# Two attention branches with a gate on one core: the first phase in another order

## The chip, the cores and the metric

The kernel runs on one core of a Trainium2 chip. The metric is the device time of one execution in microseconds (us); lower is better. PE is the matrix engine (PEld its weight loads), ACT the scalar engine, DVE the vector engine, POOL and SP two more engines, which here mostly issue DMAs.

## The reference

Two attention layers over the same 2048 x 576 input are mixed by a gate. Layer A has 32 heads of 18 columns with keys and values of their own; layer B has 32 query heads that share one key and one value of 18 columns.

```python
x = A_x                                   # 1 x 2048 x 576
g = sigmoid((x * gate_w).sum(-1, keepdims=True))
a = A(x, A_wqkv, A_wo)                    # softmax(q k^T / sqrt(18)) v per head, times wo
b = B(x, B_wq, B_wk, B_wv, B_wo)          # the same, one k and v for all heads
return g * a + (1 - g) * b                # all float32
```

## The kernel before

Products in float32 are built from halves: each operand is split into a rounded part `h` (type fp32r) and the rest `l`, and three of the four products are summed (hh, hl, lh).

The **first phase** multiplies X (transposed, 576 rows in five tiles of 128; the fifth holds the last 64 rows twice, the second copy being the rest of the split) by a matrix `wall` of 14 tiles of 128 columns, which holds key, gate, value and queries of layer B and queries and keys of layer A. X has four chunks of 512 columns. One pair of weight tile and chunk is one **bank** (`project`, one PSUM bank `ps`): 14 matmuls in the order of the list `PROJ`, 56 banks in all. ACT evicts a bank into `ph`, DVE the rest into `pl`; `ph` is stored to DRAM (`qkh`) by a DMA that ACT issues, `pl` (`qkl`) by one that POOL issues. `ph` and `pl` have three buffers each. For tiles with keys, the difference of the first two chunks is split and stored as well (`kdh`, `kdl`).

The input loads are issued by SP: `load5` brings a tile with 576 rows in three DMAs (512 rows, and the last 64 twice). First the small store of `ones` to DRAM, the first weight tile (`wst`), four X loads of 256 columns (`xs`), the second weight tile, four more X loads, four weight tiles. `split_x` makes `xh` on ACT and `xl` on DVE of 256 columns; `prep_w` makes `wh` and `wl` of a weight tile. For each chunk, tiles 0 and 1 are projected; behind them `shared_v` transposes the value of layer B on PE (L174). `project_rest` then takes tiles 2 to 13, four chunks each.

Rows of `qkh`, `qkl` and `kdh`, `kdl` are read back as operands of the attention: `ksb` and `kdb` (the shared key), `qs` (three buffers for the queries of three heads). The loads of `ksb`, `kdb` and the first head stand together on POOL behind the first eight banks in the program, those of the second and third heads behind tiles 4 and 5.

A **lead** follows the first phase: the value projection (`project_v`, L187) and the first row maxima (`step_max`, L341 and L350). Then comes the long second part, a fixed order of scores (L376), exponentials (L383), and products with the values (L390), with output projections in between. The order of the instructions of each engine is that of the program text; nothing is reordered.

Of the kernel before, what the change touches and what calls it, by code (L numbers as in the profile page):

```python
# [22 lines left out]
NKT = 5  # L23

MT = 14
ROW_KB, ROW_G, ROW_VB, ROW_Q = 0, 18, 32, 50
SCALE = DH ** -0.5
LEAD = 22
PRODS = (("h", "h"), ("h", "l"), ("l", "h"))
PROJ = [("h", "h", k, 128) for k in range(NKT)] + [("h", "l", k, 128) for k in range(NKT - 1)] + \  # L30
       [("l", "h", k, 128) for k in range(NKT)]


def q_row(u):
    return ROW_Q + DH * u if u < H else ROW_Q + DH * H + 2 * DH * (u - H)
# [7 lines left out]
def gated_mix_kernel(ctx: ExitStack, tc: tile.TileContext, xT, wall, wv, wo, out):  # L43
    nc = tc.nc
    P = 128

    def dma(o, i, eng=None):
        o, i = (x.bitcast(F32) if x.dtype == F32R else x for x in (o, i))
        return (eng or nc.sync).dma_start(o, i)  # L49
# [4 lines left out]
    ps_m = ctx.enter_context(tc.tile_pool(name="ps_m", bufs=4, space=PSUM))  # L54
# [4 lines left out]
    qk_d = [dram.tile([MT * P, S], F32, name=f"qk{x}") for x in "hl"]  # L59
    kd_d = [dram.tile([MT * P, 512], F32, name=f"kd{x}") for x in "hl"]  # L60
# [20 lines left out]
    nc.vector.memset(acc, 0.0)  # L81
    nc.vector.memset(vb, 1.0)
    nc.vector.memset(ones, 1.0)
    dma(ones_r.rearrange("a (b c) -> (a b) c", c=32), ones)

    SB, MB = 0, 64

    def load_rows(t, r, parts, eng=None):  # L90
        for b in (MB, SB):
            for i, y in enumerate(parts):
                dma(t[b + 18 * i:b + 18 * i + 18, :], qk_d[y][r:r + 18, :], eng)

    def load_q(u, eng=None):
        load_rows(qs[u % 3], q_row(u), (0, 0, 1), eng)

    def load_kd(t, r, eng=None):
        for i, y in enumerate((0, 1, 0)):
            dma(t[MB + 18 * i:MB + 18 * i + 18, :], kd_d[y][r:r + 18, :], eng)  # L100

    def load_k(t, r, eng=None):
        load_rows(t, r, (0, 1, 0), eng)


    ph1 = ExitStack()
# [1 line left out]
    wpool = ph1.enter_context(tc.tile_pool(name="wpool", bufs=2, side="right"))  # L108
    stp = ph1.enter_context(tc.tile_pool(name="stp", bufs=3, side="right"))
    X = {"h": xpool.tile([P, NKT, S], F32R, name="xh"), "l": xpool.tile([P, NKT - 1, S], F32R, name="xl")}  # L110
# [6 lines left out]
        if l is not None:  # L117
            eng_l.tensor_tensor(l, src, h.bitcast(F32), op=OP.subtract)

    def load5(t, src):  # L120
        dma(t[:, 0:4, :], src[0:512, :].rearrange("(k p) m -> p k m", p=P))
        dma(t[0:64, 4, :], src[512:576, :])
        dma(t[64:128, 4, :], src[512:576, :])

    def split_w(st, w, eng_l):
        nc.scalar.activation(w["h"], st, AF.Copy)
        eng_l.tensor_tensor(w["l"], st, w["h"].bitcast(F32), op=OP.subtract)

    def load_w(mt):
        st = wpool.tile([P, NKT, P], F32, name="wst", bufs=6)  # L130
        load5(st, wall[mt])
        return st

    def prep_w(st):
        w = {y: wpool.tile([P, NKT, P], F32R, name=f"w{y}") for y in "hl"}
        split_w(st, w, nc.vector)
        return w

    HAS_K = {0} | {k_row(u) // P for u in range(H, NU)} | {(k_row(u) + DH - 1) // P for u in range(H, NU)}
    KD = {}  # L140

    def project(mt, c, w):

        fp = ps_s.tile([P, 512], F32, name="ps")
        cs = slice(c * 512, (c + 1) * 512)
        for n, (a, b, k, kr) in enumerate(PROJ):
            nc.tensor.matmul(fp, w[a][:kr, k, :], X[b][:kr, k, cs], start=(n == 0), stop=(n == len(PROJ) - 1))  # L147
        h = stp.tile([P, 512], F32R, name="ph")
        l = stp.tile([P, 512], F32R, name="pl")
        nc.scalar.activation(h, fp, AF.Copy)  # L150
        if mt == 0 or c == 0 and mt in HAS_K:
            st = stp.tile([P, 512], F32, name="pst", bufs=3)
            nc.scalar.activation(st, fp, AF.Copy)
            if c == 0:
                KD[mt] = st
        nc.vector.tensor_tensor(l, fp, h.bitcast(F32), op=OP.subtract)  # L156
# [27 lines left out]
    def project_v(st_, hf, w):  # L184
        fp = ps_s.tile([P, 512], F32, name="ps")
        for n, (a, b, k, kr) in enumerate(PROJ):
            nc.tensor.matmul(fp[:, 0:288], X[b][:kr, k, st_ * P:(st_ + 1) * P], w[a][:kr, k, :],  # L187
                             start=(n == 0), stop=(n == len(PROJ) - 1))
        t = vst[st_ % 3]
# [3 lines left out]
    def run(gen):  # L193
        for _ in gen:
            pass

    WV = []
    with tc.tile_pool(name="xs", bufs=6, side="right") as xsp:
        W = [load_w(0)]
        XS = []  # L200

        def load_x(c):
            XS.append(xsp.tile([P, NKT, 256], F32, name="xs"))
            load5(XS[c], xT[:, 256 * c:256 * c + 256])

        def split_x(c):
            xs = XS[c]
            cs = slice(c * 256, (c + 1) * 256)
            xh = X["h"][:, :, cs]
            nc.scalar.activation(xh, xs, AF.Copy)  # L210
            nc.vector.tensor_tensor(X["l"][:, :, cs], xs[:, 0:4], xh[:, 0:4].bitcast(F32), op=OP.subtract)
            nc.vector.tensor_tensor(xh[64:128, 4], xs[64:128, 4], xh[64:128, 4].bitcast(F32), op=OP.subtract)

        for c in range(4):
            load_x(c)
        W.append(load_w(1))
        for c in range(4, 8):
            load_x(c)
        for mt in range(2, 6):
            W.append(load_w(mt))  # L220
        WP = [prep_w(W.pop(0))]
        for c in range(2):
            split_x(c)
        WP.append(prep_w(W.pop(0)))
        for c in range(4):
            if c < 3:
                split_x(2 * c + 2)
                split_x(2 * c + 3)
            keep = project(0, c, WP[0])
            project(1, c, WP[1])  # L230
            shared_v(*keep)
    vwp = ph1.enter_context(tc.tile_pool(name="vwp", bufs=1, side="right"))
    VS = [vwp.tile([P, NKT, 288], F32, name="vwst"), None]
    load5(VS[0], wv[:, 0:288])

    for b in (SB, MB):
        dma(ksb[b + 54:b + 56, :], ones_r, nc.gpsimd)
    load_k(ksb, ROW_KB, nc.gpsimd)
    load_kd(kdb, ROW_KB, nc.gpsimd)
    load_q(0, nc.gpsimd)  # L240

    def project_rest():
        WN = prep_w(W.pop(0))
        for mt in range(2, MT):
            w = WN
            if mt + 1 < MT:
                WN = prep_w(W.pop(0))
            if mt + 4 < MT:
                W.append(load_w(mt + 4))
            for c in range(4):  # L250
                project(mt, c, w)
            if mt in (4, 5):
                load_q(mt - 3, nc.gpsimd)
            if mt in (8, 11):
                hf = (mt - 8) // 3
                WV.append({y: vwp.tile([P, NKT, 288], F32R, name=f"vw{y}{hf}") for y in "hl"})
                split_w(VS[hf], WV[hf], nc.vector)
                if hf == 0:
                    VS[1] = vwp.tile([P, NKT, 288], F32, name="vwst")
                    load5(VS[1], wv[:, 288:576])  # L260

    project_rest()


    small = ctx.enter_context(tc.tile_pool(name="small", bufs=1, side="left"))
# [350 lines left out]
    for T in range(-LEAD, NSTEP + 2, 2):  # L616
# [9 lines left out]
        for op in (LEADS if T < 0 else FIRST if T == 0 else ALONE if alone else UNIT if units else PLAIN).split():  # L626
            k, second, c = op[0], op[1:2] == "B", op[2:]
# [67 lines left out]
```

## Time and profile before

| | |
|---|---|
| median of three runs | 2796.87 us (2795.1 to 2798.84) |
| the profiled execution | 2797.98 us, span 2795.9 us |
| PE, DVE, ACT busy | 99%, 87%, 87% of the span |
| mean granted PE clock | 0.995 |
| instructions | 57640 |

In the rows of a timeline the first number is the start, the second the length, both in us, then engine, line, operation, the tiles written and read, and how many were merged; in brackets stands the idle time ahead and what ended it. In a list of waits stand the sum, how often, and the longest. In rows on DMA issues the last number is the median time from issue to landing.

### The profile page before, as it was taken

To read this page: it belongs to the slowest core of one execution; us is meant where nothing else is said; L and a number is where in the kernel's file an instruction comes from. 1 tells how busy PE (TensorE), PEld (TensorE's weight loads), DVE (VectorE), ACT (ScalarE), POOL (GpSimd) and SP (SyncE) were. 2 spreads that over 40 slices of the span, in tenths; PEclk is the share of its full clock that TensorE was granted. 3 is DMA by queue.
4 is the path that set the end of the run, shared out by engine and by line. 5 is a ranking of instruction groups with operands and counts; after the bars stand their busy time and mean duration, and the time that the engine had idled before them with its cause. 6 is when DMAs were issued, how large, how long until landed. Compare 5 with 4: busy or idle time off the path is not lost.

```text
span 2795.9 us, 57640 instructions
## 1 busy us (share of the span) xinstructions
PE 2767.0 (99%) x22140; PEld 1229.2 (44%) x22140; DVE 2431.6 (87%) x4524; ACT 2430.6 (87%) x4768; POOL 207.2 (7%) x364
## 2 busy tenths in 40 slices
PE   7999999999999999999999999999999999999999
PEld 5888433333333333333333444444444443334544
DVE  3346999999999999999999999899898999998865
ACT  3231899999999999999999999999999999998775
POOL 2220000001001000100110001000100011001000
PEclk9999999999999999999999999999999999999999
DMA  8662011111112111211143223232232323233412
GB/s 258 221 230 76 27 33 33 31 47 51 40 26 57 55 32 32 64 47 26 45 101 106 70 74 104 61 85 76 80 84 76 79 71 84 63 95 107 103 36 92
DMA packets 137143, 215.09 MB, mean 77 GB/s; under 512 B 55437, under 2 KB 94301, under 8 KB 125182
## 3 DMA queue, kind: packets, MB, share of 16 engines
q1 hardware_dynamic: 116156, 168.13, 22.6%
q10 hardware_dynamic: 14120, 22.30, 2.2%
q0 software_dynamic: 6592, 20.99, 2.2%
q8 instruction: 174, 2.85, 0.4%
q14 instruction: 101, 0.83, 0.1%
HBM read 137.31 MB, written 64.77 MB: 72 GB/s over the span
## 4 chain that ended last, share of the span: by engine, by line
PE 94%; DMA 3%; DVE 2%; issue 0%; SPq 0%; ACT 0%; POOL 0%; DVEq 0%; ACTq 0%; POOLq 0%
PE ps L376 40%; PE acc L390 38%; PE ps L147 5%; PE pm L341 5%; PE pm L506 4%; PE ps L187 2%; DVE mx L350 1%; DMA xs<-xT 1%; DVE oacc L560 0%; DMA qkl<-pl 0%; SPq L49 0%; DMA ksb<-qkl 0%; DMA qs<-qkh 0%; DMA ksa<-qkh 0%; DVE oacc L514 0%
## 5 line engine op out<-in xcount | busy, mean ns | idle before, releaser
L383 ACT ACTIVATE pt<-ps 128x512 f32<-128x512 f32 x4052 | 2128.6, 612 | 108.2 <-PE pm L341 45.6
L350 DVE TENSOR_REDUCE mx<-pm 128x1 f32<-128x512 f32 x3096 | 1975.9, 683 | 168.0 <-PE pm L341 126.7
L376 PE MATMUL ps<-qs,ksb 56*128 56x512 f32 x2688 | 908.2, 437 | 0.0
L341 PE MATMUL pm<-ksb,qs 54*128 54x512 f32 x2364 | 825.5, 446 | 1.1 <-DVE mx L350 0.3
L376 PEld LDWEIGHTS ps<-qs,ksb 56*128 56x128 f32 x2688 | 437.0, 184 | 685.2 <-ACT pt L383 665.1
L390 PE MATMUL acc<-pt,vb 128*19 128x256 f32 (+1 forms) x6144 | 592.5, 457 | 0.1
L390 PE MATMUL acc<-pt,vg 128*19 128x256 f32 (+1 forms) x5656 | 579.3, 481 | 0.7 <-DVE oe L400 0.4
L376 PE MATMUL ps<-qs,ksa 56*128 56x512 f32 x1364 | 455.7, 437 | 0.0
L341 PE MATMUL pm<-ksa,qs 54*128 54x512 f32 x1232 | 433.5, 443 | 0.0
L341 PEld LDWEIGHTS pm<-ksb,qs 54*128 54x128 f32 x2364 | 379.5, 184 | 10.6 <-DVE mx L350 4.1
L376 PEld LDWEIGHTS ps<-qs,ksa 56*128 56x128 f32 x1364 | 218.2, 184 | 342.9 <-ACT pt L383 316.8
L347 DVE CUSTOM_DVE_ANT_0 junk<-pm,xb 128x512 bf16<-128x512 f32 x500 | 339.9, 680 | 0.0
L344 ACT ACTIVATE xb<-pm 128x512 f32<-128x512 f32 x500 | 305.1, 610 | 0.0
L341 PEld LDWEIGHTS pm<-ksa,qs 54*128 54x128 f32 x1232 | 200.3, 184 | 0.9
L390 PEld LDWEIGHTS acc<-pt,vb 128*19 128x19 f32 x6144 | 104.2, 97 | 209.9 <-issue 199.9
L390 PEld LDWEIGHTS acc<-pt,vg 128*19 128x19 f32 x5656 | 95.9, 97 | 209.0 <-issue 197.7
L341 PE MATMUL pm<-kdb,qs 54*128 54x512 f32 x372 | 148.6, 400 | 0.0
L116 POOL CAST mh<-mt 128x32 fp32r<-128x32 f32 x64 | 13.4, 209 | 1683.4 <-DVE mt L358 1683.4
L156 DVE TENSOR_TENSOR pl<-ps,ph 128x512 fp32r<-128x512 f32 x56 | 38.4, 690 | 98.1 <-ACT ph L150 70.2
L150 ACT ACTIVATE ph<-ps 128x512 fp32r<-128x512 f32 x56 | 33.4, 597 | 102.4 <-PE ps L147 87.4
L147 PE MATMUL ps<-xh,wh 128*128 128x512 f32 x280 | 75.6, 401 | 20.9 <-ACT xh L210 13.4
L147 PE MATMUL ps<-xh,wl 128*128 128x512 f32 x280 | 73.5, 393 | 0.0
(99 smaller groups left out, 1334.7 us busy)
## 6 DMA issues: line engine op xcount, KB each, us to landing
qs<-qkh SPq DMA_DIRECT2D x244, 144.0 KB
qs<-qkl SPq DMA_DIRECT2D x122, 144.0 KB
qkh<-ph ACTq DMA_DIRECT2D x56, 256.0 KB
qkl<-pl POOLq DMA_DIRECT2D x56, 256.0 KB, 3.1
ksa<-qkh SPq DMA_DIRECT2D x88, 144.0 KB
onh<-oh SPq DMA_DIRECT2D x32, 256.0 KB
onl<-ol SPq DMA_DIRECT2D x32, 256.0 KB
oih<-onh SPq DMA_DIRECT2D x16, 512.0 KB
```

The lines of the kernel that those rows point to most:

```text
L147: nc.tensor.matmul(fp, w[a][:kr, k, :], X[b][:kr, k, cs], start=(n == 0), stop=(n == len(PROJ) - 1))
L150: nc.scalar.activation(h, fp, AF.Copy)
L156: nc.vector.tensor_tensor(l, fp, h.bitcast(F32), op=OP.subtract)
L187: nc.tensor.matmul(fp[:, 0:288], X[b][:kr, k, st_ * P:(st_ + 1) * P], w[a][:kr, k, :], start=(n == 0), stop=(n == len(PROJ) - 1))
L341: nc.tensor.matmul(pm, qs[u % 3][b:b + 54, i * P:(i + 1) * P], k, start=True, stop=True)
L344: nc.scalar.activation(MX["x", u, i], pm, AF.Relu)
L347: nc.vector.tensor_tensor_reduce(junk, pm, MX.pop(("x", u, i)), 1.0, -3e38, op0=OP.add, op1=OP.max, accum_out=MX[u][:, i, c:c + 1])
L350: nc.vector.tensor_reduce(MX[u][:, i, c:c + 1], pm, axis=AX.X, op=OP.max)
L376: nc.tensor.matmul(ps, kst(u)[b:b + 56, i * P:(i + 1) * P], qs[u % 3][b:b + 56, c * 512:(c + 1) * 512], start=True, stop=True)
L383: nc.scalar.activation(pt, ps, AF.Exp, scale=SCALE)
L390: nc.tensor.matmul(acc[32 * j:32 * j + 19, a:b], v_of(u, i), PT[u, i, j][:, a:b], start=(i == 0), stop=(i == 15), skip_group_check=True)
L506: nc.tensor.matmul(fp[:, 0:288], o[b][:r, t, s2 * P:(s2 + 1) * P], w[a][:r, t, 288 * hf:288 * hf + 288], start=(n == 0), stop=(n == 3 * nt ...
```

## The change

- `PROJ` has the order hh, lh, hl for the first four row tiles, and the fifth at the end. `load5` maps row 4p+k instead of 128k+p to partition p of row tile k, for X, `wall` and `wv` alike.
- The first weight tile is issued by ACT, behind a copy of `ones` onto itself on ACT; the first X load is SP's first DMA; the small parts of the second X load and of the second weight tile, and the third weight tile, are issued by POOL. The store of `ones` is issued behind the X loads. X is loaded in two pieces of 256 columns and three of 512.
- Three weight tiles instead of two are projected for each chunk, and `wh` and `wl` have three buffers. The split of the next chunk stands behind the second tile. The first bank is computed in two halves of 256 columns.
- Five matmuls of 304 columns on the identity and a constant tile are put ahead of the first bank; their result is not used.
- The row loads of `ksb`, `kdb` and the first three heads are put into a list, and one is issued on POOL behind each bank from tile 3 on. The load of `wv` moves to tile 5.

```diff
-PROJ = [("h", "h", k, 128) for k in range(NKT)] + [("h", "l", k, 128) for k in range(NKT - 1)] + \
-       [("l", "h", k, 128) for k in range(NKT)]
+PROJ = [(a, b, k, 128) for a, b in (("h", "h"), ("l", "h"), ("h", "l")) for k in range(NKT - 1)] + \
+       [("h", "h", NKT - 1, 128), ("l", "h", NKT - 1, 128)]
...
-    dma(ones_r.rearrange("a (b c) -> (a b) c", c=32), ones)
+    nc.scalar.activation(ones, ones, AF.Copy)
...
-    def load5(t, src):
-        dma(t[:, 0:4, :], src[0:512, :].rearrange("(k p) m -> p k m", p=P))
-        dma(t[0:64, 4, :], src[512:576, :])
-        dma(t[64:128, 4, :], src[512:576, :])
+    def load5(t, src, eng=None, rest=None):
+        dma(t[:, 0:4, :], src[0:512, :].rearrange("(p k) m -> p k m", p=P), eng)
+        dma(t[0:64, 4, :], src[512:576, :], rest or eng)
+        dma(t[64:128, 4, :], src[512:576, :], rest or eng)
...
-        for n, (a, b, k, kr) in enumerate(PROJ):
-            nc.tensor.matmul(fp, w[a][:kr, k, :], X[b][:kr, k, cs], start=(n == 0), stop=(n == len(PROJ) - 1))
+        g = 512 // parts
+        for i in range(parts):
+            for n, (a, b, k, kr) in enumerate(PROJ):
+                nc.tensor.matmul(fp[:, g * i:g * i + g], w[a][:kr, k, :],
+                                 X[b][:kr, k, c * 512 + g * i:c * 512 + g * i + g],
+                                 start=(n == 0), stop=(n == len(PROJ) - 1))
...
+    warm = ps_m.tile([P, 512], F32, name="pm")
+    for i in range(5):
+        nc.tensor.matmul(warm[:, 0:304], ident, vst[0].rearrange("p h d -> p (h d)"), start=True, stop=True)
+    rows_back = []
+    def bring_row():
+        if rows_back:
+            rows_back.pop(0)()
+    def later(o, i, eng):
+        rows_back.append(lambda: dma(o, i, nc.gpsimd))
...
-        for c in range(4):
-            load_x(c)
-        W.append(load_w(1))
-        for c in range(4, 8):
-            load_x(c)
-        for mt in range(2, 6):
+        W = [load_w(0, nc.scalar)]
+        load_x(0)
+        load_x(1, nc.gpsimd)
+        W.append(load_w(1, nc.scalar, nc.gpsimd))
+        W.append(load_w(2, nc.gpsimd))
+        for c in range(2, 5):
+            load_x(c)
+        dma(ones_r.rearrange("a (b c) -> (a b) c", c=32), ones)
+        for mt in range(3, 6):
             W.append(load_w(mt))
         WP = [prep_w(W.pop(0))]
-        for c in range(2):
-            split_x(c)
+        split_x(0)
+        split_x(1)
+        WP.append(prep_w(W.pop(0)))
         WP.append(prep_w(W.pop(0)))
         for c in range(4):
+            keep = project(0, c, WP[0], 2 if c == 0 else 1)
+            if c == 3:
+                WN = prep_w(W.pop(0))
+            project(1, c, WP[1])
             if c < 3:
                 split_x(2 * c + 2)
                 split_x(2 * c + 3)
-            keep = project(0, c, WP[0])
-            project(1, c, WP[1])
             shared_v(*keep)
+            project(2, c, WP[2])
...
-    load_k(ksb, ROW_KB, nc.gpsimd)
-    load_kd(kdb, ROW_KB, nc.gpsimd)
-    load_q(0, nc.gpsimd)
+    load_k(ksb, ROW_KB, put=later)
+    load_kd(kdb, ROW_KB, put=later)
+    for u in range(3):
+        load_q(u, put=later)
...
+        for mt in range(3, MT):
...
+            if mt == 5:
+                load_wv(0)
             for c in range(4):
                 project(mt, c, w)
-            if mt in (4, 5):
-                load_q(mt - 3, nc.gpsimd)
+                bring_row()
```

More of the change, by code (lines that the diff above doesn't have):

```diff
@@ L83, in gated_mix_kernel, with load_rows, load_q, load_kd @@
     nc.vector.memset(ones, 1.0)
-    dma(ones_r.rearrange("a (b c) -> (a b) c", c=32), ones)
+    nc.scalar.activation(ones, ones, AF.Copy)
     SB, MB = 0, 64
-    def load_rows(t, r, parts, eng=None):
+    def load_rows(t, r, parts, put=dma):
         for b in (MB, SB):
             for i, y in enumerate(parts):
[L93 to L98, printed above, removed]
+                put(t[b + 18 * i:b + 18 * i + 18, :], qk_d[y][r:r + 18, :], None)
+    def load_q(u, put=dma):
+        load_rows(qs[u % 3], q_row(u), (0, 0, 1), put)
+    def load_kd(t, r, put=dma):
         for i, y in enumerate((0, 1, 0)):
-            dma(t[MB + 18 * i:MB + 18 * i + 18, :], kd_d[y][r:r + 18, :], eng)
-    def load_k(t, r, eng=None):
-        load_rows(t, r, (0, 1, 0), eng)
+            put(t[MB + 18 * i:MB + 18 * i + 18, :], kd_d[y][r:r + 18, :], None)
+    def load_k(t, r, put=dma):
+        load_rows(t, r, (0, 1, 0), put)
     ph1 = ExitStack()
@@ L127, in split_w, with load_w @@
         eng_l.tensor_tensor(w["l"], st, w["h"].bitcast(F32), op=OP.subtract)
-    def load_w(mt):
+    def load_w(mt, eng=None, rest=None):
         st = wpool.tile([P, NKT, P], F32, name="wst", bufs=6)
-        load5(st, wall[mt])
+        load5(st, wall[mt], eng, rest)
         return st
     def prep_w(st):
-        w = {y: wpool.tile([P, NKT, P], F32R, name=f"w{y}") for y in "hl"}
+        w = {y: wpool.tile([P, NKT, P], F32R, name=f"w{y}", bufs=3) for y in "hl"}
         split_w(st, w, nc.vector)
@@ L140, in gated_mix_kernel, with project @@
     KD = {}
-    def project(mt, c, w):
+    def project(mt, c, w, parts=1):
         fp = ps_s.tile([P, 512], F32, name="ps")
         cs = slice(c * 512, (c + 1) * 512)
-        for n, (a, b, k, kr) in enumerate(PROJ):
-            nc.tensor.matmul(fp, w[a][:kr, k, :], X[b][:kr, k, cs], start=(n == 0), stop=(n == len(PROJ) - 1))
+        g = 512 // parts
[4 more added lines that the diff above has]
+                                 start=(n == 0), stop=(n == len(PROJ) - 1))
         h = stp.tile([P, 512], F32R, name="ph")
@@ L195, in run, with load_x @@
             pass
+    warm = ps_m.tile([P, 512], F32, name="pm")
[7 more added lines that the diff above has]
+        rows_back.append(lambda: dma(o, i, nc.gpsimd))
     WV = []
-    with tc.tile_pool(name="xs", bufs=6, side="right") as xsp:
-        W = [load_w(0)]
+    VS = [None, None]
+    with tc.tile_pool(name="xs", bufs=1, side="right") as xsp:
         XS = []
-        def load_x(c):
-            XS.append(xsp.tile([P, NKT, 256], F32, name="xs"))
-            load5(XS[c], xT[:, 256 * c:256 * c + 256])
+        def load_x(c, rest=None):
+            half = c < 2
+            XS.append(xsp.tile([P, NKT, 256 if half else 512], F32, name=f"xs{half}", bufs=2))
+            load5(XS[c], xT[:, 256 * c:256 * c + 256] if half else xT[:, 512 * (c - 1):512 * c], None, rest)
         def split_x(c):
-            xs = XS[c]
+            xs = XS[c // 2 + 1][:, :, 256 * (c % 2):256 * (c % 2) + 256] if c > 1 else XS[c]
             cs = slice(c * 256, (c + 1) * 256)
@@ L228, in gated_mix_kernel, with load_wv, project_rest @@
                 split_x(2 * c + 3)
-            keep = project(0, c, WP[0])
-            project(1, c, WP[1])
             shared_v(*keep)
+            project(2, c, WP[2])
     vwp = ph1.enter_context(tc.tile_pool(name="vwp", bufs=1, side="right"))
-    VS = [vwp.tile([P, NKT, 288], F32, name="vwst"), None]
-    load5(VS[0], wv[:, 0:288])
+    def load_wv(hf):
+        VS[hf] = vwp.tile([P, NKT, 288], F32, name="vwst")
+        load5(VS[hf], wv[:, 288 * hf:288 * hf + 288])
     for b in (SB, MB):
-        dma(ksb[b + 54:b + 56, :], ones_r, nc.gpsimd)
-    load_k(ksb, ROW_KB, nc.gpsimd)
-    load_kd(kdb, ROW_KB, nc.gpsimd)
-    load_q(0, nc.gpsimd)
-    def project_rest():
-        WN = prep_w(W.pop(0))
-        for mt in range(2, MT):
+        later(ksb[b + 54:b + 56, :], ones_r, None)
+    load_k(ksb, ROW_KB, put=later)
+    load_kd(kdb, ROW_KB, put=later)
+    for u in range(3):
+        load_q(u, put=later)
+    def project_rest(WN):
+        for mt in range(3, MT):
             w = WN
@@ L247, in project_rest @@
                 WN = prep_w(W.pop(0))
-            if mt + 4 < MT:
-                W.append(load_w(mt + 4))
+            if mt + 3 < MT:
+                W.append(load_w(mt + 3))
+            if mt == 5:
+                load_wv(0)
             for c in range(4):
                 project(mt, c, w)
-            if mt in (4, 5):
-                load_q(mt - 3, nc.gpsimd)
+                bring_row()
             if mt in (8, 11):
@@ L258, in project_rest @@
                 if hf == 0:
-                    VS[1] = vwp.tile([P, NKT, 288], F32, name="vwst")
-                    load5(VS[1], wv[:, 288:576])
-    project_rest()
+                    load_wv(1)
+        assert not rows_back
+    project_rest(WN)
     small = ctx.enter_context(tc.tile_pool(name="small", bufs=1, side="left"))
```

## The prediction

> **What bounds the kernel now.** I read the page's busy times first, then the table of windows, the timeline of each engine where PE is idle, the chain, and the waits and DMA issues of single stretches.
>
> ```profile
> PE 2767.0 (99%) x22140; PEld 1229.2 (44%) x22140; DVE 2431.6 (87%) x4524; ACT 2430.6 (87%) x4768; POOL 207.2 (7%) x364
> ```
>
> ```profile
> 0.00:13.36 13.36, 0.00 (x0) 0.00 (x1) 3.33 (x7) 4.56 (x4) 1.56 (x9) 1.00 0.58 180
> ...
> 71.67:207.49 135.82, 135.82 (x590) 112.29 (x591) 52.22 (x73) 43.85 (x70) 34.60 (x65) 0.98 0.65 226
> 207.49:2795.90 2588.41, 2581.51 (x21341) 1077.75 (x21339) 2352.10 (x4410) 2361.49 (x4665) 155.76 (x261) 1.00 0.24 64
> ```
>
> In the windows the first number is the length, the second PE's busy time. PE is idle for 28.9 us (2795.9 - 2767.0), and 13.4 of these lie before the first matmul; from 71.67 to 207.49 it never stops. The first phase (56 banks of 14 matmuls, L147) ends at 207.49, where the chain goes over to the first L187 matmul (its row stands below). The change touches nothing behind that point, so I ask only when the first phase ends after it.
>
> PE at its own pace needs this for a bank:
>
> ```profile
> 47.52 1.45 PE L147 MATMUL ps<-xh,wh 128*128 128x512 f32 x5 [2.73 <-ACT wh L126]
> ```
>
> ```profile
> 71.67 2.50 PE L147 MATMUL ps<-xh,wh 128*128 128x512 f32 x5 [4.78 <-DVE pl L156]
> ...
> 77.22 1.30 PE L147 MATMUL ps<-xh,wh 128*128 128x512 f32 x5
> ```
>
> ```profile
> 118.47 1.30 PE L147 MATMUL ps<-xh,wh 128*128 128x512 f32 x5
> ```
>
> From 77.22 to 118.47 are 13 banks: 3.173 us each, so 56 banks are 177.7 us. The first phase lasts 29.8 us longer than that. The bank at 71.67 takes 5.55 us (to 77.22), 2.4 too many, after 4.78 us idle; the one at 47.52, after 2.73 us idle, runs at the usual pace. So an idle PE loses its clock somewhere between these two lengths and pays 2.4 us to get it back.
>
> ```profile
> 13.36 2.51 PE L147 MATMUL ps<-xh,wh 128*128 128x512 f32 x5 [13.36 <-ACT xh L210]
> ...
> 19.05 1.33 PE L147 MATMUL ps<-xh,wh 128*128 128x512 f32 x5
> ...
> 22.71 1.43 PE L147 MATMUL ps<-xh,wh 128*128 128x512 f32 x5
> ```
>
> The first bank lasts from 13.36 to 19.05, 2.5 us over the pace. The next, with a transpose group behind it, ends at 22.71: 3.66, so a group costs 0.5, four of them 2.0. The 29.8 us are then: start 13.4, two cold banks 4.9, the stall at 66.89 4.8, the wait for the third weight tile at 47.52 2.7, transposes 2.0, and 2.0 left for small waits for splits.
>
> **The start.** These are SP's issues and its wait ahead of the first, then ACT, then DVE, up to 14 us:
>
> ```profile
> 1.83 0.35 SPq L49 DMA_DIRECT2D ones_r<-ones  x1
> 2.24 1.75 SPq L49 DMA_DIRECT2D wst<-wall  x3
> 4.03 7.55 SPq L49 DMA_DIRECT2D xs<-xT  x12
> ```
>
> ```profile
> SPq L49 <- DVE ones L83: 1.2, 1, 1.2
> ```
>
> ```profile
> 5.96 1.28 ACT L126 ACT_TABLE_LOAD   x1 [5.96 <-DMA wst<-wall]
> 7.25 0.74 ACT L126 ACTIVATE wh<-wst 128x640 fp32r<-128x640 f32 x1
> 8.81 1.27 ACT L210 ACTIVATE xh<-xs 128x1280 fp32r<-128x1280 f32 x1 [0.82 <-DMA xs<-xT]
> 12.04 1.27 ACT L210 ACTIVATE xh<-xs 128x1280 fp32r<-128x1280 f32 x1 [1.96 <-DMA xs<-xT]
> ```
>
> ```profile
> 1.71 0.09 DVE L83 MEMSET ones<- 128x32 f32 x1
> 8.02 0.82 DVE L127 TENSOR_TENSOR wl<-wst,wh 128x640 fp32r<-128x640 f32 x1 [6.22 <-ACT wh L126]
> 10.11 1.23 DVE L211 TENSOR_TENSOR xl<-xs,xh 128x1024 fp32r<-128x1024 f32 x1 [1.27 <-ACT xh L210]
> 11.37 0.42 DVE L212 TENSOR_TENSOR xh<-xs,xh 64x256 fp32r<-64x256 f32 x1
> ```
>
> SP waits 1.2 us for the memset of ones before its first issue, then issues the first weight tile, and reaches X only at 4.03; the first X tile has landed 4.78 us later, at 8.81. Without that wait it could begin with X at 0.6; I take 0.9, so it can land at 5.7. The weight tile is issued by ACT, behind the copy of ones (memset ends at 1.80, copy short, table load beside it): about 2.4. Before it took 3.7 us from 2.24 to 5.96, so now it lands at 6.1. The table load (1.28) no longer stands behind that. ACT: weights 6.1 to 6.9, first half of X 6.9 to 8.2. ACT also issues the second weight tile in between, which as built waits for the first X load; that is there by then. First real matmul 8.3 instead of 13.36, since the first bank is now two halves of 256 columns, and only half of X is needed. Bounds: 7.5, if the loads land a microsecond earlier than before for lack of a queue ahead of them; and 10.1, the end of the present xh at 8.81, if three queues bring nothing earlier.
>
> What the halves cost shows in the chain's row of matmuls with 288 columns and weights of the same shape:
>
> ```profile
> 207.49 3.70 PE ps L187 x28
> ```
>
> 0.132 us each, so 14 with 256 columns are at most 1.85 us, a pair of halves 3.7 instead of 3.17. But the second half waits for its own data. DVE has wl, xl, the lower tile, xl, the lower tile (0.82, 1.23, 0.42, 1.23, 0.42) from 6.9 on: with ACT's first half ending at 8.2, the first xl ends at 9.4, and the new order of PROJ puts the products with xl behind eight others, so the first half bank runs from 8.3 to 10.3. The small parts of the second X tile come by Pool's queue:
>
> ```profile
> 1.24 0.93 POOL L182 MEMSET vst<- 128x304 f32 x3
> ```
>
> ```profile
> L49 POOL DMA_DIRECT2D qkl<-pl x41 | 22.2, 541 | 86.1 <-DVE pl L156 86.0 <-issue 0.2
> ```
>
> Pool is free at 2.2 and issues two in 1.1 us; with the 5.9 us from issue to landing that this queue needs at a moderate load (row below) they are there at 9.2, with the 11.2 of its worst row below at 14.5. I take 5.9, since little else is on the queue yet: ACT copies from 9.2 to 10.5, xl ends at 11.7, the lower tile at 12.1, and bank one at 12.5, against 19.05. With 14.5 it ends at 17.7 (1.27, 1.23, 0.42 and the last two matmuls behind it), the late bound.
>
> The idle matmuls are five plain float32 ones of 304 columns on identity and a memset tile. The nearest row:
>
> ```profile
> L390 PE MATMUL acc<-pt,vb 128*19 128x256 f32 (+1 forms) x6144 | 592.5, 457 | 0.1
> ```
>
> 457 ns for 256 columns gives 543 ns for 304, and twice that at the slow clock: 2.7 to 5.4 us from about 1.6 on, over by 7.0 at the latest. So they stand in nobody's way and leave 1 to 4 us idle before 8.3. By the two gaps above (2.73 kept the clock, 4.78 lost it) the first bank should find a fast clock in most cases: 2.4 us saved, 0 at worst.
>
> The Trainium skill, "TensorE: Matmul & The Clock Gate", Part 1, says that the clock is gated to half until one window of about 3.4 us has been busy, and is gated again after an idle one, the windows running free. The trace agrees: 3.4 lies between 2.73 and 4.78. By this rule a gap over 3.4 us here would make the matmuls useless; that is a rival below.
>
> **Three tiles a chunk.** A chunk of 512 columns of X now feeds three banks, 9.5 us and a transpose, instead of two, 6.3. Between chunks PE needs two ACT copies (2.54), two pairs on DVE (3.3) and the evictions. ACT does the copies behind the eviction of the second tile, so they run beside the third bank: they end at 12.5 + 3.2 + 0.6 + 0.3 + 2.5 = 19.1, and the third bank, with a transpose group ahead of it, at 19.3. The lower halves come 2 us later, but the order of PROJ needs them 1.8 us after the bank begins. So at most some tenths for each of three chunks. Weight tiles two and three are prepared before the first bank, tile four at chunk 3, two banks ahead of its use: the 2.73 us at 47.52 goes.
>
> What can come late are the loads of X:
>
> ```profile
> DMA  9999999999999999899798999989999285059999
> GB/s 343 261 272 270 346 320 345 354 326 376 348 361 335 307 284 323 237 277 274 251 303 198 354 340 397 478 277 292 376 422 347 75 314 182 23 205 220 234 285 306
> DMA packets 6246, 6.51 MB, mean 296 GB/s; under 512 B 530, under 2 KB 5026, under 8 KB 6245
> ```
>
> That is the DMA view from 20 to 42 us, in 40 slices: the 16 DMA engines are full (9 tenths or more) in most. Up to the last X tile (needed near 36) come 5.2 MB of X, 1.0 MB of weights and some 4.2 MB of stores: 10.4 MB, at 296 GB/s 35 us, from 2.4 on: 37.6, 1.6 us late. The new loads have longer pieces (rows p*4+k are neighbours, so a weight piece is 2 KB instead of 512 B, X of a whole chunk 2 KB instead of 1 KB), so I expect more than 296. I take 1.0 us for all waits in this stretch, bounds 0 and 6.
>
> **Rows for the lead.** Now 17 loads (2 of ones, 6 and 3 of the shared key, 6 of the first head) stand in a row on Pool, ahead of the stores of pl of the next banks:
>
> ```profile
> DVE pl L156 <- DMA qkl<-pl: 12.2, 1, 12.2
> ...
> PE ps L147 <- DVE pl L156: 4.8, 1, 4.8
> ```
>
> DVE waits 12.2 us for a buffer of pl, PE therefore 4.8, plus 2.4 cold. With one load behind each bank of tile 3 and on, 29 of them, Pool issues a store, then one row. The nearest rows are the loads of two heads at 95 and 108 us, six in a row on the same queue (DMA view from 93 to 120 us):
>
> ```profile
> qkl<-pl POOLq DMA_DIRECT2D x8, 256.0 KB, 5.7
> qs<-qkh POOLq DMA_DIRECT2D x8, 144.0 KB, 5.9
> ```
>
> PE never stops there (fully busy from 71.67 to 207.49). As built, each Pool load waits for the one eight before it. With a store, a row and a quarter of kdl a bank, eight last 3.173 * 8 / 2.25 = 11.3 us; 5.9 is well inside. The stall of 7.2 us goes at no cost; all rows come from tile 0 and are in by tile 10. Loads of weights and of wv are early as before.
>
> **The sum.** Bank one ends at 12.5. The other 55 banks: 174.5. Transposes 2.0, waits 1.0, and 0.6 for the bank after a transpose, which starts 0.14 slower (1.43 against 1.30). End of the first phase 190.6 instead of 207.49: 16.9 us less. The profiled execution took 2797.98 us (span 2795.9), so 2781.1; its time lies 1.1 over the median 2796.87, from which it would be 2780.0. I forecast 2780.
>
> **The rivals.** A: the data comes late. By the Trainium skill, "DMA: Bandwidth & Descriptors", Issuing engines are not separate DMA queues, loads issued from several engines share the same 16 DMA engines, and it only saves the issuing time. As a mechanism here: the three first issuers only share out what SP alone moved, the second X tile lands at 12.04 as now and the first bank ends at 15 (1.27, 1.23 and 0.42 later) instead of 12.5, and the X tiles at the 296 GB/s of the row come 1.6 us late twice: 2.5 + 3.2 = 5.7, so 2786. For it speak the full slices from 20 us on; against it that the DMA share before 13.36 is only 0.58 (last but one number of the first window) and that SP reaches X at 4.03. If one wait passes 3 to 4 us, 2.4 for the clock comes on top: 2788.
>
> B: the idle matmuls do not hold the clock (over too early, at 4.3, and the first bank late). Cost 2.4: 2783. For it: 543 ns at full speed would end them by 4.3, four microseconds before 8.3; against: they begin cold.
>
> C, slower: the rows spread over 29 banks hold up each bank, not only one spell. If a load on Pool's queue takes longer than 11.3 us, Pool is late with each next store, DVE waits for pl and PE for the bank. To be slower by over 5.6 us it must eat 16.9 + 5.6 = 22.5 us, 0.78 a bank, so loads must take (3.17 + 0.78) * 8 / 2.25 = 14.0 us. From there on it is over 2802.5. For it: in the present burst (DMA view from 46 to 72 us) a load took this:
>
> ```profile
> kdb<-kdl POOLq DMA_DIRECT2D x1, 36.0 KB, 11.2
> ```
>
> Against: 5.9 at the pace of a few in between, and PE unharmed by six in a row.
>
> D: the second part gives it back. It is ordered by hand and its engines wait for nothing of the first; I see no row for that, but a remainder.
>
> **How the numbers follow.** Forecast 0.62, with its own range 2776 to 2783; A 0.2 (2784 to 2789); B 0.1; C 0.03; D 0.05, of which most within 0.2%. 0.2% is 5.6 us, about what a measurement of this kernel can tell from no change (runs from 2795.1 to 2798.84). Early bound: start at 7.5 and no waits, 1.8 us less than the sum, and as much again for the runs' own spread (1.8 below the median): 2776. The forecast's own range, B and most of A lie up to 2788. Faster by more than 0.2% needs only 5.6 of the 16.9 us: the forecast, A, B, and a little of D, 0.93; same 0.04; slower 0.03.
>
> **What would show it.** In the profile after: first L149 matmul near 8.3; tile 0's second half done near 12; no idle PE over 1 us from there to the first L191 matmul near 190; that one bank in three has the transposes; DVE's wait for qkl stores gone; from L191 on the same length to the end, 2588.4 us. Wrong would be: PE idle for pl between 45 and 140 us (C), ACT idle for xs at the second or third chunk (A), a first bank in matmuls of 0.2 us and more after the data is there (B), or a longer rest behind the first L191 (D).

## The result, and the profile after

The changed kernel takes 2792.67 us (median of 22 runs, 2790.59 to 2795.58) against 2797.04 us before (22 runs): ratio 0.9984, 95% interval 0.9978 to 0.999. It is faster by 4.4 us; 2780 had been forecast. The profiled execution (2795.58 us) was the slowest of the 22.

The table of windows of the changed kernel, cut where PE stops and where the first phase ends (the last three numbers of a row are PE's granted clock, the busy share of the DMA engines and GB/s):

```profile
0.00:11.84 11.84, 4.73 (x11) 3.00 (x11) 1.68 (x5) 3.46 (x5) 5.43 (x16) 0.88 0.78 254
11.84:17.01 5.17, 5.17 (x28) 5.17 (x29) 4.50 (x6) 2.47 (x3) 0.00 (x0) 0.62 1.06 284
17.01:34.40 17.39, 17.39 (x80) 13.31 (x78) 8.61 (x13) 7.03 (x10) 3.27 (x6) 1.00 0.67 214
34.40:40.35 5.95, 0.00 (x1) 0.00 (x1) 1.18 (x1) 2.48 (x3) 0.00 (x0) 0.94 0.83 316
40.35:60.39 20.04, 20.04 (x79) 15.64 (x79) 10.16 (x16) 7.29 (x11) 2.70 (x5) 0.85 0.64 207
60.39:203.43 143.04, 143.04 (x632) 118.49 (x633) 54.07 (x76) 46.67 (x75) 44.60 (x83) 1.00 0.71 243
203.43:2793.80 2590.37, 2583.37 (x21341) 1080.43 (x21339) 2352.00 (x4410) 2361.72 (x4665) 155.84 (x261) 0.99 0.24 64
```

The first phase ends at 203.43 instead of 207.49: 4.06 us, close to the 4.4 of the medians. The rest takes 2590.4 against 2588.4; over all profiles of this document its length lies between 2587.7 and 2590.4. The stall at 66.89 is gone: PE is busy throughout from 40.35 to 203.43. The second window shows the first bank at a granted clock of 0.62. A stop of 5.95 us at 34.40 is new, and the bank behind it is slow: it lasts from 40.35 to 46.49, 6.1 us where a bank at pace takes 3.2. The timeline of PE marks both stops:

```profile
1.64 4.73 PE L204 MATMUL pm<-vst,ident 128*128 128x304 f32 x10 [1.64 <-POOL vst L186]
11.84 1.22 PE L149 MATMUL ps<-xh,wh 128*128 128x256 f32 x4 [5.47 <-ACT xh L230]
40.35 2.08 PE L149 MATMUL ps<-xh,wh 128*128 128x512 f32 x4 [5.95 <-ACT xh L230]
...
46.49 1.09 PE L149 MATMUL ps<-xh,wh 128*128 128x512 f32 x4
```

Both waits are for xh, a copy of ACT. ACT's timeline ahead of the first one (rows of ACTq are DMAs that ACT issues):

```profile
1.84 0.39 ACTq L49 DMA_DIRECT2D wst<-wall  x1
...
9.89 0.74 ACT L126 ACTIVATE wh<-wst 128x640 fp32r<-128x640 f32 x1 [7.65 <-DMA wst<-wall]
10.53 2.41 ACT L230 ACTIVATE xh<-xsTrue 128x1280 fp32r<-128x1280 f32 x2
```

The first weight tile, issued at 1.84, is there at 9.89: 8.0 us, where the prediction had 3.7 us and a landing at 6.1. Ahead of the second stop:

```profile
30.00 0.33 ACTq L49 DMA_DIRECT2D qkh<-ph  x1
30.60 0.33 ACTq L49 DMA_DIRECT2D kdh<-pdh  x1
30.97 0.34 ACTq L49 DMA_DIRECT2D z_d<-pst  x1
31.41 0.60 ACT L154 ACTIVATE ph<-ps 128x512 fp32r<-128x512 f32 x1 [0.83 <-PE pm L178]
37.43 0.33 ACTq L49 DMA_DIRECT2D qkh<-ph  x1
37.87 2.43 ACT L230 ACTIVATE xh<-xsFalse 128x1280 fp32r<-128x1280 f32 x2 [5.86 <-DMA qkh<-ph]
```

ACT has evicted the bank at 32.0 and then does nothing until 37.43, when it issues the store of that bank; the copies of the next chunk stand behind it in its order. The chain names what ended that wait, the store issued at 30.00:

```profile
30.00 7.36 DMA qkh<-ph
37.87 2.44 ACT xh L230 x2
```

That store is there at 37.36 (30.00 + 7.36), and the issue behind it starts at 37.43. In the program as built, the two stores share one of eight completion counters, and an issue waits until the DMA that used its counter last has landed (ACT's instructions, numbered in its order):

```
24 L49 DMACopy qkh<-ph 128x512 [waits DMAHW5_49,Activation_49]
...
28 L49 DMACopy qkh<-ph 128x512 [waits DMAHW5_49,Activation_49]
29 L230 Activation xh<-xsFalse 128x5x256 [waits DMAHW4_49,DMAHW3_49]
```

### The profile page after: what moved, and what is told of

Read it like the earlier page. It is cut to its first block, busy times and chain, and to the rows that moved or that the text cites. A ratio compares the mean times of both kernels' runs of the same rounds, so it can differ in the third digit from the quotient of the medians.

```text
span 2793.8 us, 57690 instructions
## 1 busy us (share of the span) xinstructions
PE 2773.7 (99%) x22164; PEld 1236.0 (44%) x22164; DVE 2432.2 (87%) x4524; ACT 2431.1 (87%) x4769; POOL 211.8 (8%) x371
## 4 chain that ended last, share of the span: by engine, by line
PE 96%; DVE 2%; DMA 1%; ACT 0%; SPq 0%; issue 0%; DVEq 0%; POOL 0%; ACTq 0%
PE ps L406 41%; PE acc L420 38%; PE ps L149 6%; PE pm L371 5%; PE pm L536 4%; PE ps L191 2%; DVE mx L380 1%; DVE oacc L590 0%; DMA qs<-qkl 0%; DVE oacc L544 0%; DMA xsTrue<-xT 0%; DMA qkh<-ph 0%; PE pm L406 0%; SPq L49 0%; DMA qs<-qkh 0%; DVE oe L430 0%
## 5 line engine op out<-in xcount | busy, mean ns | idle before, releaser
L149 PE MATMUL ps<-xh,wh 128*128 128x512 f32 (+1 forms) x285 | 85.1, 397 | 11.4 <-ACT xh L230 11.4
L149 PE MATMUL ps<-xh,wl 128*128 128x512 f32 (+1 forms) x285 | 83.8, 392 | 0.0
```

The costliest lines, as they stand in the source:

```text
L149: nc.tensor.matmul(fp[:, g * i:g * i + g], w[a][:kr, k, :], X[b][:kr, k, c * 512 + g * i:c * 512 + g * i + g], start=(n == 0), stop=(n == ...
```

## The experiments

All are edits of the changed kernel unless said; the ends come from each kernel's profile, the ratios are to the kernel before. PE's first matmul of L149 (L147 in the kernel before), the end of the first bank, later stops of PE in the first phase, its end:

| kernel | first | bank one | later stops | phase ends | ratio (95% interval) |
|---|---|---|---|---|---|
| before | 13.36 | 19.05 | 1.1, 2.7, 4.8 | 207.49 | 1 |
| changed | 11.84 | 17.01 | 5.95 | 203.43 | 0.9984 (0.9978 to 0.999) |
| copies_first | 10.99 | 16.63 | 2.1, 0.7 | 198.76 | 0.9972 (0.9961 to 0.9982) |
| pool_stores | 10.68 | 15.63 | none | 192.75 | 0.9958 (0.9944 to 0.9972) |
| few_loads_first | 10.28 | 15.29 | 5.8 | 200.23 | 0.998 (0.9971 to 0.9988) |
| single_queue | 8.83 | 14.33 | 6.1 | 199.84 | 0.9977 (0.9968 to 0.9986) |
| idle_11 | 11.46 | 16.45 | 6.3 | 203.40 | 0.9986 (0.9977 to 0.9995) |
| no_idle_matmuls | 10.84 | 16.29 | 6.0 | 201.50 | 0.9985 (0.9976 to 0.9993) |
| rows_burst | 10.88 | 16.86 | 5.5, 5.0 | 209.79 | 1.0005 (0.9996 to 1.0014) |
| before_rows_spread | 13.38 | 18.67 | 1.4, 3.2 | 202.11 | 0.9991 (0.9982 to 1.0) |
| one_queue_pool_stores | 9.50 | 13.42 | none | 190.56 | 0.9943 (0.993 to 0.9956) |
| whole_first_bank | 11.29 | 14.60 | none | 191.73 | 0.9954 (0.9941 to 0.9968) |
| two_tiles | 8.69 | 13.35 | 2.7, 0.5 | 193.91 | 0.9962 (0.995 to 0.9975) |

Kernels that begin with the same code and loads differ by up to 1.2 us in the first matmul (10.68 to 11.84), so smaller differences there say nothing.

**The stop at 34 us.** First the order was turned round:

```diff
...
+        if ahead is not None:
+            ahead()
         dma(qk_d[0][mt * P:(mt + 1) * P, cs], h, nc.scalar)
...
```

`ahead` is the split of the next chunk, for the second tile of the first three chunks.

> The changed kernel with one order turned round: in the second tile's bank of each chunk, ACT's two copies of the next chunk stand ahead of the issue of that bank's ph store instead of behind it; the transfers are the same. Theory (issue wait): in the changed kernel ACT stood from 32.0 to 37.4 us in front of the issue of a ph store, which waits for an earlier ph store to land, and the copies stood behind it; so the idle PE of 5.95 us at 34.4 and the slow bank behind it go, the first phase ends about 8 us earlier (near 195), and the time falls by about 8 us, to near 2785. Rival (data late): the third X piece itself lands only near 37, the copies wait for it instead, the idle time at 34.4 stays over 4 us, and the time stays within 2 us of the changed kernel.

The stop fell from 5.95 to 2.1 us and the phase ended 4.7 us earlier, little more than half of what was expected. ACT's timeline shows the rest:

```profile
30.08 0.33 ACTq L49 DMA_DIRECT2D kdh<-pdh  x1
32.73 0.24 ACTq L49 DMA_DIRECT2D z_d<-pst  x1
33.02 0.60 ACT L154 ACTIVATE ph<-ps 128x512 fp32r<-128x512 f32 x1 [2.98 <-DMA xsFalse<-xT]
33.52 2.42 ACT L232 ACTIVATE xh<-xsFalse 128x1280 fp32r<-128x1280 f32 x2
```

Now the issue of the gate row, 2 KB, holds ACT until 32.73, for a load of X on its counter. That piece of X is not the one the copies need: theirs was issued by 11.1, the one on the counter at 25.29. So every DMA issue on ACT can be such a wait. Then those of tiles 0 to 2 were all taken away, also the ones of `kd_d[0]` and `z_d`:

```diff
-        dma(qk_d[0][mt * P:(mt + 1) * P, cs], h, nc.scalar)
+        by = nc.gpsimd if mt < 3 else nc.scalar
+        dma(qk_d[0][mt * P:(mt + 1) * P, cs], h, by)
...
```

> The changed kernel with the stores of tiles 0 to 2 (ph, the key difference, the gate row) issued by Pool instead of ACT, so that ACT issues no DMA between the copies of the X chunks; the same bytes move. With the copies put ahead of one store issue, the idle time at 34 us had gone from 5.95 to 2.1 us, and what was left was the gate row's issue, which waited on ACT from 30.4 to 32.7 for a load of X. Theory (issue wait on ACT): no idle time of PE over 0.5 us between the first bank and the end of the first phase, no slow bank, end near 195, 8 us earlier than the changed kernel. Rival (data late, or full DMA engines): the stores are as slow as before on Pool, ph buffers come free late, ACT waits for them, and 2 to 6 us of idle time stay.

PE has no stop left after its first matmul, and the phase ends 10.7 us earlier, 1.4 of it by the earlier first bank. The same bytes move. From 24 to 40 us the DMA engines are even fuller than in the changed kernel (5.16 MB against 4.09), and a store of `ph` still takes 5.7 us to land (median), yet PE does not stop. So neither late data nor full DMA engines alone made the stop: it was ACT waiting to issue. PE's rows of the first bank and the chain's row at the end:

```profile
10.68 1.17 PE L149 MATMUL ps<-xh,wh 128*128 128x256 f32 x4 [3.61 <-ACT xh L231]
```

```profile
192.75 3.71 PE ps L192 x28
```

**The start.** Two steps towards one queue:

```diff
-        load_x(1, nc.gpsimd)
-        W.append(load_w(1, nc.scalar, nc.gpsimd))
-        W.append(load_w(2, nc.gpsimd))
+        load_x(1)
+        W.append(load_w(1))
+        W.append(load_w(2))
```

> The changed kernel, but only the first weight tile is issued by ACT; both first X pieces and then weight tiles two and three are issued by SP one after the other, none by Pool, and the large X pieces come behind them. Theory (shared engines): the first weight tile took 8.0 us from issue to use because loads of three queues shared the DMA engines; with fewer beside it it is there at 6 to 7 instead of 9.89, and the first real matmul starts at 8.5 to 9.5 instead of 11.84. The second bank may wait for weight tile two. End of the first phase 2 to 3 us earlier. Rival (slow queue): ACT's queue is slow with its first loads whatever runs beside it, then the first copy stays near 9.9 and the first matmul near 11.8, and the phase ends no earlier, or later, because the tiles come one after the other.

The first copy began at 8.33 and the first matmul at 10.28, later than expected but 0.4 us ahead of the earliest profile with three queues; that is less than the 1.2 us above, so this step alone shows little. The stop stayed (5.8). Then the first weight tile went to SP as well:

```diff
-        W = [load_w(0, nc.scalar)]
+        W = [load_w(0)]
```

> The changed kernel with all first loads issued by SP one after the other: weight tile one, X piece one and two, weight tiles two and three, large X pieces; nothing is issued by ACT or Pool. With fewer loads at once the first weight tile had landed at 8.33 instead of 9.89 and the first matmul at 10.28 instead of 11.84. Theory (shared engines): one queue in the order of need is faster still: weight tile at 4.5 to 5.5, X piece one at 7 to 8, first matmul at 8.5 to 9.5, first phase 2 to 3 us shorter than in the changed kernel. Rival (issue time): SP's six issues of 0.6 us ahead of X's end cost what the order wins, first matmul at 10 to 11, and weight tile two comes late, so that the second bank waits 1 us and more.

ACT's timeline:

```profile
4.05 0.74 ACT L126 ACTIVATE wh<-wst 128x640 fp32r<-128x640 f32 x1 [1.81 <-DMA wst<-wall]
7.51 1.27 ACT L230 ACTIVATE xh<-xsTrue 128x1280 fp32r<-128x1280 f32 x1 [2.73 <-DMA xsTrue<-xT]
```

The weight tile is there at 4.05, 5.8 us earlier than in the changed kernel, X at 7.51, and the first matmul at 8.83. Three queues move more in the first 12 us and yet bring the first tile later; the DMA view of 0 to 12 us, the changed kernel first, then one_queue_pool_stores, which has the loads of single_queue:

```profile
DMA packets 2293, 3.05 MB, mean 255 GB/s; under 512 B 224, under 2 KB 1504, under 8 KB 2293
```

```profile
DMA packets 2343, 2.41 MB, mean 200 GB/s; under 512 B 241, under 2 KB 1905, under 8 KB 2343
```

The 3.05 MB hold what is not yet needed (weight tiles two and three, the large X piece); in single_queue what is needed first is issued first and was there first. Whether sharing alone made the tile late is not shown: with only SP's loads beside it (few_loads_first) it still took 6.5 us (1.84 to 8.33), and no run issues it on ACT with nothing else in flight, so a slowness of ACT's own queue is not excluded. The phase still ends at 199.84, since the stop at 34 us is 6.1 us here.

**The idle matmuls.**

```diff
-    for i in range(5):
+    for i in range(11):
```

That is idle_11; no_idle_matmuls has `range(0)`.

> The changed kernel with 11 idle matmuls instead of 5. In the changed kernel the five lasted 4.7 us, ended at 6.4, and 5.5 us idle followed; the first half bank ran at 0.22 to 0.3 us a matmul. Theory (clock lost in the gap): eleven last to about 12, the first half bank runs at 0.13, and the first bank ends at 15.5 to 16 instead of 17.0, bound by the splits on DVE; 1 to 1.5 us less in the first phase. Rival (no effect): the first half bank is bound by ACT and DVE anyway, and its end stays at 17.0; or the last idle matmul ends later than 11.84 and the bank ends later.

> The changed kernel without the five idle matmuls. In it they ended 3.2 to 5.5 us before the first bank, and the first half bank ran slowly all the same. Theory (they are over too early): first half bank at 0.21 us a matmul as with them, first bank done within 0.5 us of 17.0 plus or minus the 0.6 by which the first loads differ between profiles; time within 1 us of the changed kernel. Rival (they help in part): without them the whole first bank and some of the second are slow, the first bank ends 1.5 to 2.4 us later after its start than with them, and the time is that much longer.

Neither eleven nor none moved the time. Eleven ended at 9.3, not at 12, since they sped up on the way:

```profile
1.64 7.68 PE L204 MATMUL pm<-vst,ident 128*128 128x304 f32 x22 [1.64 <-POOL vst L186]
11.46 0.74 PE L149 MATMUL ps<-xh,wh 128*128 128x256 f32 x4 [2.14 <-ACT xh L230]
12.04 0.98 PE L149 MATMUL ps<-xh,wl 128*128 128x256 f32 x4
12.82 1.13 PE L149 MATMUL ps<-xl,wh 128*128 128x256 f32 x4
```

After 2.14 us idle the first four are fast and the next ones slow. From start to end the first bank lasts 5.0 us here, 5.45 without idle matmuls, 4.95 to 5.98 with five. As the change has them, they bought nothing that could be measured.

**The rows.** One part undone in the changed kernel, and done alone in the kernel before:

```diff
-        rows_back.append(lambda: dma(o, i, nc.gpsimd))
+        dma(o, i, nc.gpsimd)
...
```

That is rows_burst: the loads stand together behind the chunks again, those of the second and third heads behind tiles 4 and 5.

> The changed kernel with one part undone: the 17 row loads of the shared key and the first head stand together on Pool behind the chunks, those of the second and third heads behind tiles 4 and 5, as before. Theory (rows step right): PE stops again for 4 to 5 us near 70 us and loses its clock (2.4 us), the first phase ends 6 to 8 us later than in the changed kernel (203.4), at 210, and the time is that of before plus 2 to 4 us. Rival: with three tiles in the chunk loop the stores are further ahead, the burst costs under 3 us, and the rows step gave little here.

> The kernel before with one part of the change alone: the loads of rows for the lead one behind each bank from tile 3 on. Theory (rows step right): the idle PE of 4.8 us at 66.89 and the slow bank behind it go, and the first phase ends 7.2 us earlier, at about 200.3; time 0.9974 of before, near 2790. Rival (a new wait): loads spread over 29 banks hold up stores of pl, PE shows idle times between 60 and 150 us, and the phase ends less than 4 us earlier.

With the burst, PE stops at 81.4 for 5.04 us, for pl, and begins cold; the phase ends 6.4 us later, and the ratios' intervals (0.9996 to 1.0014, and 0.9978 to 0.999 without the burst) do not overlap. PE's timeline and the waits from 40 to 90 us:

```profile
86.42 2.08 PE L149 MATMUL ps<-xh,wh 128*128 128x512 f32 x4 [5.04 <-DVE pl L160]
```

```profile
DVE pl L160 <- DMA qkl<-pl: 12.5, 1, 12.5
```

In the kernel before, spreading took away the stop at 66.89 (7.2 us with its cold bank) but the phase ended only 5.4 us earlier: the wait for weight tile three happened to be 3.21 us instead of 2.73, and this time the clock was lost (0.66 from 47.87 to 52.90), which gave 2 us back:

```profile
47.87 2.09 PE L147 MATMUL ps<-xh,wh 128*128 128x512 f32 x5 [3.21 <-ACT wh L126]
```

In time it was only 2796.15 to 2794.52 us by the medians, where near 2790 had been expected, and the interval of its ratio reaches 1.0; the rest of its profile is 2590.0 us long.

**Together.** Single_queue, pool_stores and 10 idle matmuls in one kernel:

> Three edits at once in the changed kernel: first loads all by SP in the order of need, stores of tiles 0 to 2 by Pool, 10 idle matmuls instead of 5. Theory: the first matmul at 8.5 to 9.5, the first bank done near 13.5, no idle time behind it, so 13.5 + 174.5 + 2.6 + 0.5 = 191: the end that the prediction had (190.6); 12 us less than the changed kernel in the first phase, time near 2781. Rival: one of the two waits comes back in another place (a bank waiting for weight tile two or for the second X chunk), and the phase ends at 194 or later.

```profile
1.64 8.25 PE L205 MATMUL pm<-vst,ident 128*128 128x304 f32 x20 [1.64 <-POOL vst L187]
```

```profile
9.50 0.86 PE L149 MATMUL ps<-xh,wh 128*128 128x256 f32 x4
...
13.42 1.09 PE L149 MATMUL ps<-xh,wh 128*128 128x512 f32 x4
```

```profile
190.56 3.71 PE ps L192 x28
```

The idle matmuls run to 9.9 by their row, the first bank follows without a gap and fast, and the phase ends at 190.56. The median is 2780.82 us (5 runs, 2779.99 to 2782.15), the fastest of all kernels here. From this version two parts of the change were undone, the halves (`2 if c == 0 else 1` left out) and the third tile (its banks behind the chunks; splits ahead of the bank of tile 0, in the first chunk behind it):

> The fastest version (first loads all by SP in the order of need, stores of tiles 0 to 2 by Pool, 10 idle matmuls), with the first bank in one piece of 512 columns instead of two halves. There the halves ran from 9.5 to 11.4 and from 11.4 to 13.4 without a gap. Theory: the whole bank starts when the second piece's copy is done (11.3), takes 3.2 to 3.5 and ends at 14.6 to 14.8; after the idle matmuls' end at 9.9 stand 1.4 us, so the clock may be partly lost; first phase 1.2 to 2.4 us longer, time near 2782. Rival: the halves are bound by the second piece anyway and the bank ends within 0.5 us of 13.4.

> The fastest version with two weight tiles a chunk instead of three: tile 2's four banks come behind the four chunks, and the splits of a chunk stand ahead of the tile 0 bank of the chunk before it, as in the kernel before. Theory (X supply): chunks are needed every 6.7 us instead of 9.9, the third large piece waits for a buffer and comes late; PE idles 3 to 8 us in all between 15 and 45 us, and the first phase ends at 194 to 199 instead of 190.6. Rival: X is there in time with one queue in order, no idle time over 1 us, end within 1.5 us of 190.6: three tiles then give nothing that order and queues do not.

The whole bank starts at 11.29 and ends at 14.60; the phase is 1.2 us longer. With two tiles PE waits once for 2.69 us and the phase is 3.4 us longer, just under what was expected; the wait is for the first large piece of X, not the third as expected. PE's row, then ACT's:

```profile
19.75 1.19 PE L149 MATMUL ps<-xh,wh 128*128 128x512 f32 x4 [2.69 <-ACT xh L231]
```

```profile
17.27 2.43 ACT L231 ACTIVATE xh<-xsFalse 128x1280 fp32r<-128x1280 f32 x2 [2.64 <-DMA xsFalse<-xT]
```

## Why the prediction was wrong, by its own steps

The time lies above the forecast's range (2776 to 2783) and above every end that rival A was given (2788). By the prediction's own measure of 5.6 us the 4.4 us are no change, to which it had given 0.04. Two terms of its sum failed, the start and the waits between chunks.

- **That only the first phase changes:** right. The gain of the medians (4.4) is near that of the phase (4.06, one profile each).
- **The start (8.3 forecast, 11.84 measured; first bank at 12.5, measured 17.01): the term that failed first, by 4.5 us.** The late bound of the start (10.1) was passed too: it allowed for a late X, not for a late weight tile. I priced that tile at the 3.7 us that it had taken at the head of the one queue, and gave it to ACT beside loads from two other queues. That was near rival A's first half, by which the queues only share out what one moved; but A had the second X tile late, not the weight tile, and the bank at 15. The profiled execution is the slowest of its 22; the five other profiles that begin alike have the first matmul at 10.68 to 11.46 and the bank at 15.63 to 16.86, so the miss is 3.1 to 4.5 us. The Trainium skill, "DMA: Bandwidth & Descriptors", Issuing engines are not separate DMA queues, says that DMAs of several engines run on the same 16 DMA engines and interleave. The runs agree as far as they go: 8.0 us for the tile with three queues, 6.5 with two, 3.3 (0.72 to 4.05) with one.
- **The idle matmuls: rival B came true.** Their length was right (4.73, forecast 2.7 to 5.4), but the late start left 5.47 us behind them and the clock was at 0.62 for the first bank. It cost about 1 us (a first bank of 5.17 us instead of 4.2), not the 2.4 that B had.
- **Waits between chunks (1.0 forecast, bounds 0 and 6): the larger failure, 5.95 us and a cold bank that took 3.0 more than one at pace.** I counted ACT's copies behind the eviction and one issue of 0.3 us, and never asked what that issue waits for. It was not late data, as rival A's second half had it: with the stores on another engine, all X pieces were in time. The chain of the kernel before had shown the same kind of wait, and I read past it:

```profile
29.94 3.54 DMA qkh<-ph
33.56 0.33 ACTq L49
33.89 0.05 issue
33.93 1.28 ACT xh L210
```

- **Rows:** right. Undoing them cost 6.4 us in the phase, against the 7.2 priced, and rival C did not come: landings of 2.9 to 4.4 us for these loads in the changed kernel are far inside 11.3.
- **Halves and three tiles:** right in direction; undone in the fastest version, they cost 1.2 and 3.4 us of the phase in one profile each. The prediction gave neither a price of its own except the 2.73 us of the wait for weight tile three, and with two tiles it was X that came late.
- **The sum:** 12.5 + 174.5 + 2.0 + 1.0 + 0.6 nearly held when both waits were out: 13.42 + 177.14 = 190.56, where 190.6 stood, and 2780.8 us, where 2780 stood. That it is so close is in part luck: the first bank was 0.9 later than forecast, and the 1.0 for waits did not come; and it is a kernel with other queues and more idle matmuls than the one forecast. In the changed kernel the error was in the two terms, 4.5 and 7.9 (5.95 and 3.0, less the 1.0), and some tenths.

What stays open is how often the unprofiled runs have the stop at 34 us; the changed kernel and each of its variants with the copies behind ACT's stores had it in the profile, at 5.5 to 6.3 us.

## What to carry to other kernels

An engine that both computes and issues DMAs can stand at an issue until an earlier DMA has landed, as ACT did here for 5.4 us (32.0 to 37.43). Ahead of work on the critical path, look for issues on that engine in the instruction order, ask which transfer each one waits for, and give stores to an engine that nobody waits for. With the first loads on three queues the one that was needed first came at 9.89, with all of them in one queue in the order of need at 4.05. What some steps save, a new wait behind them can take back: here 4.4 us came from the change as it was, and 16 us when the queue of the first loads, the engine of the stores and the number of idle matmuls were changed as well.

## What the runs showed of the hardware that I had not expected

The clock does not go by the length of a gap alone. By the granted clock in the windows behind them, gaps of 3.21 us (before_rows_spread, 0.66), 2.14 (idle_11, 0.75 and then 0.63) and 2.12 (copies_first, 0.62) lost it; gaps of 2.73 (before) and 2.69 (two_tiles) did not (1.00). After 1.76 us in single_queue eight matmuls were fast (1.00 until 10.09), and then the clock fell (0.60 until 14.33), with PE at work:

```profile
8.83 0.74 PE L149 MATMUL ps<-xh,wh 128*128 128x256 f32 x4 [1.76 <-ACT xh L230]
9.41 0.63 PE L149 MATMUL ps<-xh,wl 128*128 128x256 f32 x4
10.09 0.87 PE L149 MATMUL ps<-xl,wh 128*128 128x256 f32 x4
10.76 0.41 PE L149 MATMUL ps<-xh,wh 128*128 128x256 f32 x1
```

The Trainium skill, "TensorE: Matmul & The Clock Gate", Part 1, says that the clock is gated again after at least one idle window of about 3.4 us, the windows running free. These runs do not agree: gaps of 2.14 and 1.76 us are too short to hold such a window, and the clock fell all the same. It was not settled why 1.76 us was enough in one profile and 2.73 us was not in another.

The column of the granted clock misleads ahead of the first change that a trace holds: it reads 1.00 for the first bank of no_idle_matmuls (10.84 to 16.29), though the matmuls from 11.87 to 13.57 take 0.21 us each and those from 15.58 to 16.06 take 0.12. There the length of the matmuls is the better sign.
